# Exchanging the filler work of two stages, with fewer and larger transposing loads, in a fused forward and backward kernel

## The chip, the cores and the metric

The kernel runs on one core of a Trainium2 chip. The metric is the device time of one execution in microseconds (us). SBUF is the memory on the core, PSUM the small one, in banks, in which the matmuls leave their sums. The granted clock is the share of full speed at which PE was let run, as the profile records it. Engines are named as the profile names them: PE (matmul; PEld is its weight load), DVE (VectorE), ACT (ScalarE), POOL (GpSimd) and SP (SyncE, which issues most DMAs here; "SPq" is its queue). A program on one core has no die to compare, so a run of several rounds is called fast when it lies within 1.5% of the fastest of its kernel.

## The reference

The reference is the forward pass and all gradients of `x + A(LN(x)) + B(LN(x))` for S = 2048 rows, D = 512 columns, F = 1376 hidden columns, in bf16:

```python
def _A_ref(q, k, v, shift_k, ssm_k, ssm_D):
    k_shift = ...                       # causal 4-tap convolution of k with shift_k
    kv = k_shift * v
    y = irfft(rfft(kv padded to 4096) * rfft(ssm_k padded to 4096))[:2048] + kv * ssm_D
    return q * y
def _B_ref(x, w_gate, w_up, w_down):
    return ((x @ w_gate) * (x @ w_up)) @ w_down
xn = layernorm(x)
out = x + _A_ref(xn, ...) + _B_ref(xn, ...)   # and jax.vjp for all nine inputs
```

Ten outputs: out_0 the result; out_1, out_2, out_3 the gradients of x, k, v (2048 x 512); out_4 of shift_k (512 x 4); out_5 of ssm_k (512 x 2048); out_6 of ssm_D (512 numbers); out_7, out_8, out_9 of the three MLP weights.

## The kernel before

The long convolution is done as matmuls with generated sine tables. The program has four parts, and two of them are *paired*: the instruction streams of two independent jobs are woven together, so that PE always has matmuls of one job while the other waits for ACT or DVE.

1. MLP forward (`pg`, `pd`) over 8 chunks of 256 rows, with the first transform step (`pa`) between. It leaves three hidden tensors of every chunk in DRAM (`HDD`) and the transformed rows in DRAM (`AX`).
2. The **spectral step** (`pX`, pointwise products on DVE, `pC`), which reads `AX` and writes `CX`, paired with the **MLP backward matmuls** (`po`, `px`, 528 matmuls of 512 columns), which reread `HDD` chunk by chunk and leave their results in SBUF.
3. The **output stage** (`py`, `p5`, `psD` and most of the elementwise work), which reads `CX`, paired with the **weight gradients** (`pw`, 560 matmuls), which need the hidden tensors with rows and columns exchanged: 9 groups, each of 8 transposing loads.
4. The end of the output stage.

```python
def nat_load(n):                                  # transposing loads of group n
    t, g = glist[n]; fb0, nf = GRP[g]             # GRP = [(0, 4), (4, 4), (8, 3)] blocks of 128
    dst = f["nat"][n % 2]
    for ch in range(NCH):                         # 8 loads of 192 to 256 KB
        ldT(out=dst[:, ch, 0:nf, :]..., in_=HDD[ch, :, t, fb0:fb0 + nf, :]...)
...
st(HDD[ch], hd[ch % 2][:])                        # part 1: one store of a chunk, 16.9 KB per partition
...
while not SG.done:                                # part 2: spectral step + MLP backward
    SG(1)
    Y(5)
Y(1000)
f_alloc(); c_load(0)
nat_load(0)
while not (WG.done and CG.done):                  # part 3: weight gradients + output stage
    WG(12)
    CG(1)
```

At the end of the output stage, two outputs are stored element by element, and the sums for out_2 use one buffer:

```python
def dk_pair(r0):                                  # 4 products, 3 sums, one store of 256 KB
    dks = f["dks"]; acc = f["dk"]; ...
    st(o2[:, r0:r0 + 2, :], acc[:])
...
st(out_5.rearrange("(q p) s -> p q s", p=128), o5[:])
st(out_6.rearrange("(q p) -> p q", p=128), dD)            # 512 pieces of 2 bytes
st(out_4.rearrange("(q p) j -> p q j", p=128), ds4)       # 512 pieces of 8 bytes
```

## Time and profile before

| | kernel before |
|---|---|
| median at first (4 runs) | 617.23 us (613.73 to 619.96) |
| profiled span | 618.2 us |
| PE busy, DVE busy, ACT busy | 498.6, 357.1, 325.0 us |
| DMA | 146.85 MB, mean 238 GB/s |

The page of the kernel before has a row for each engine in which a digit is the busy share of one fortieth of the span, in tenths, and below them the granted PE clock and the DMA engines in the same form:

```profile
PE 498.6 (81%) x3040; PEld 258.0 (42%) x3084; DVE 357.1 (58%) x706; ACT 325.0 (53%) x403; POOL 7.7 (1%) x20
...
PE   0399999999998999999999989379699887795300
...
PEclk9999999999999999999999999879799989897655
DMA  8967867976956849756748997838999999987710
```

PE is full, or nearly, from the third slice to the twenty-fifth, then has holes, and the clock falls with them. The windows view gives busy time by stretch. Columns: window, its length, busy us (and instructions) of PE, PEld, DVE, ACT, POOL, then the granted clock, the mean busy share of the 16 DMA engines, and GB/s. A share above 1 comes from packet records that overlap, and is read as full. The four rows are part 1, part 2, part 3 until PE's last main work, and the end. They are cut by eye: the last matmuls of part 2 run to 362 us, and the last of the output stage, which wait for DVE, to 586:

```profile
core 0: us, PE busy (x) PEld busy (x) DVE busy (x) ACT busy (x) POOL busy (x), PEclk, DMA share, GB/s
0.00:184.50 184.50, 153.40 (x1340) 127.34 (x1358) 142.12 (x298) 130.12 (x199) 6.75 (x19) 1.00 0.79 270
184.50:356.00 171.50, 166.98 (x864) 53.94 (x879) 89.38 (x161) 111.84 (x126) 0.00 (x0) 1.00 0.73 248
356.00:577.00 221.00, 173.90 (x827) 75.92 (x837) 104.09 (x207) 79.39 (x75) 0.95 (x1) 0.90 0.91 231
577.00:618.20 41.20, 4.31 (x12) 0.76 (x11) 21.56 (x42) 3.63 (x4) 0.00 (x0) 0.50 0.23 84
```

Part 2 is bound by PE with DMA at 0.73. In part 3 PE idles 47 of 221 us, the clock is 0.90, and DMA is at 0.91 while it moves *fewer* bytes per second than in part 1. In the last 41 us there is hardly a matmul. The waits view (engine, line and tile, what it waited for; us in total, times, longest) names what PE waited for in part 3, and the timeline of the SP queue (start, us, line, what) shows why: eight transposing loads stand in front of the loads of the output stage.

```profile
PE py L602 <- DMA big<-CX: 27.0, 7, 13.4
...
PE psD L648 <- DVE big L646: 14.9, 9, 4.3
...
PE pw L712 <- DMA big<-HDD: 5.1, 6, 1.6
```

```profile
507.42 11.21 SPq L685 DMA_TRANSPOSE big<-HDD  x8
518.68 0.57 SPq L635 DMA_DIRECT2D out_dram<-big  x1
519.35 0.38 SPq L653 DMA_DIRECT2D out_dram<-big  x1
519.78 1.29 SPq L567 DMA_DIRECT2D big<-CX  x2
```

### The profile page before, as it was taken

The page shows a single profiled execution, that of the slowest core. Times are in us where ns is not written, and L with a number is a line of the kernel's source. Part 1 is how long each engine was busy: PE and PEld are TensorE (multiplying, and loading weights), DVE is VectorE, ACT ScalarE, POOL GpSimd, SP SyncE. Part 2 cuts the span into 40 slices and gives each one's busy share as a digit, 9 for nine tenths or more (in the row PEclk, how much of TensorE's full clock was granted, in tenths as well). Part 3 has the DMA queues.
Part 4 walks back from the last instruction along what each step waited for, and adds up shares of the span by engine and source line. Part 5 has one row for each costly group of instructions (what it writes and reads, how often), then busy time and mean ns, then how long its engine had stood idle before and what let it go on. Part 6 is the DMA issues. An engine that isn't in the chain of part 4 may idle for free. (4 is left out here: it accounts for less than half of the span.)

```text
span 618.2 us, 8204 instructions
## 1 busy us (share of the span) xinstructions
PE 498.6 (81%) x3040; PEld 258.0 (42%) x3084; DVE 357.1 (58%) x706; ACT 325.0 (53%) x403; POOL 7.7 (1%) x20
## 2 busy tenths in 40 slices
PE   0399999999998999999999989379699887795300
PEld 0297778787783333333333334133234423342100
DVE  4477999877863746464646317034266471639970
ACT  2076888789974866666666515042235340515500
POOL 2000010000000000000000000000000000000000
PEclk9999999999999999999999999879799989897655
DMA  8967867976956849756748997838999999987710
GB/s 294 329 135 279 316 232 287 372 282 200 313 193 278 312 162 317 261 203 242 290 151 290 226 295 179 181 99 184 276 239 255 302 201 223 261 241 279 273 43 9
DMA packets 124007, 146.85 MB, mean 238 GB/s; under 512 B 90240, under 2 KB 96192, under 8 KB 122047
## 3 DMA queue, kind: packets, MB, share of 16 engines
q1 hardware_dynamic: 122764, 142.99, 75.8%
q10 hardware_dynamic: 1202, 3.34, 1.5%
q8 instruction: 24, 0.39, 0.3%
q14 instruction: 17, 0.13, 0.1%
HBM read 65.30 MB, written 59.28 MB: 202 GB/s over the span
## 5 line engine op out<-in xcount | busy, mean ns | idle before, releaser
L712 PE MATMUL pw<-big 128*128 128x512 bf16 (+1 forms) x384 | 88.2, 379 | 7.8 <-DMA big<-HDD 5.1
L352 PE MATMUL pg<-big 128*128 128x256 bf16 (+1 forms) x704 | 88.9, 273 | 0.5
L352 PEld LDWEIGHTS <-big 128*128 128x128 bf16 (+1 forms) x704 | 69.5, 100 | 13.2 <-issue 0.2
L449 PE MATMUL px<-big 128*128 128x512 bf16 (+1 forms) x172 | 65.4, 380 | 0.9 <-issue 0.8
L447 PE MATMUL px<-big 128*128 128x512 bf16 (+1 forms) x169 | 64.3, 381 | 0.5 <-issue 0.5
L484 DVE TENSOR_TENSOR big<-big 128x2048 bf16<-128x2048 bf16 x16 | 19.6, 1225 | 76.2 <-ACT big L477 76.2
L477 ACT CAST big<-pX 128x1024 bf16<-128x1024 f32 x48 | 48.4, 1013 | 26.2 <-PE pX L476 19.0
L615 DVE TENSOR_TENSOR big<-big 128x1024 bf16<-128x1024 bf16 x8 | 5.5, 693 | 97.4 <-ACT big L603 97.4
L353 ACT CAST big<-pg 128x512 bf16<-128x512 f32 (+1 forms) x88 | 52.0, 604 | 17.3 <-PE pg L352 16.2
L508 ACT CAST big<-pC 128x1024 bf16<-128x1024 f32 x48 | 48.6, 1012 | 23.3 <-PE pC L507 20.8
L712 PEld LDWEIGHTS <-big 128*128 128x128 bf16 x384 | 37.4, 101 | 54.8 <-issue 23.9
L400 ACT CAST big<-pa 128x1024 bf16<-128x1024 f32 x48 | 48.2, 1034 | 5.2 <-PE pa L399 2.2
L359 PE MATMUL pd<-big 128*128 128x256 bf16 (+1 forms) x352 | 47.2, 273 | 1.0 <-ACT big L353 0.7
L441 PE MATMUL po<-big 128*128 128x512 bf16 (+1 forms) x169 | 44.1, 381 | 0.8 <-issue 0.6
L603 ACT CAST big<-py 128x1024 bf16<-128x1024 f32 x16 | 15.5, 1015 | 54.2 <-PE py L602 54.1
L716 ACT CAST big<-pw 128x512 bf16<-128x512 f32 (+1 forms) x24 | 14.5, 620 | 55.4 <-PE pw L712 37.0
L699 PE MATMUL pw<-big 128*128 128x512 bf16 (+1 forms) x172 | 42.0, 394 | 0.5 <-issue 0.4
L602 PE MATMUL py<-big 128*128 128x512 bf16 x58 | 19.7, 450 | 27.6 <-DMA big<-CX 27.0
L611 ACT CAST big<-p 128x1024 bf16<-128x1024 f32 x8 | 36.8, 4595 | 2.9 <-PE p L609 2.9
L359 PEld LDWEIGHTS <-big 128*128 128x128 bf16 (+1 forms) x352 | 34.8, 100 | 7.9 <-issue 0.9
L364 DVE TENSOR_TENSOR big<-big 128x1024 bf16<-128x1024 bf16 (+1 forms) x48 | 30.7, 640 | 4.4 <-ACT big L361 4.3
L648 PE MATMUL psD<-big 128*32 128x512 bf16 x64 | 20.7, 439 | 14.9 <-DVE big L646 14.9
(116 smaller groups left out, 662.5 us busy)
## 6 DMA issues: line engine op xcount, KB each, us to landing
HDD<-big SPq DMA_DIRECT2D x8, 2112.0 KB, 9.1
big<-HDD SPq DMA_DIRECT2D x6, 2112.0 KB, 8.9
AX<-big SPq DMA_DIRECT2D x16, 768.0 KB, 4.2
big<-AX SPq DMA_DIRECT2D x16, 768.0 KB, 5.1
CX<-big SPq DMA_DIRECT2D x16, 768.0 KB, 4.8
big<-CX SPq DMA_DIRECT2D x16, 768.0 KB, 6.1
out_dram<-big SPq DMA_DIRECT2D x32, 256.0 KB, 2.8
big<-in_A_v_dram SPq DMA_DIRECT2D x16, 256.0 KB, 7.9
```

What stands on the lines that cost most here:

```text
L352: MM(pg[:fw, j, :], lhsT=W[:, c, fb * 128:fb * 128 + fw], rhs=T[:, 0, c, :], start=(c == 0), stop=(c == 3))
L353: ACOPY(g[:fw, 0:2, i, :], pg[:fw])
L359: MM(pd[:fw, i, :], lhsT=WdT[:, c, fb * 128:fb * 128 + fw], rhs=T[:, 1, c, :], start=(c == 0), stop=(c == 3))
L400: ACOPY(a[:, :, t, :], pa[:])
L441: MM(po[:], lhsT=h[:fw, 0, fb, ss], rhs=wy["d"][:fw, fb, :], start=(fb == 0), stop=(fb == NFB - 1))
L447: MM(px[:], lhsT=h[:fw, 1, fb, ss], rhs=wy["g"][:fw, fb, :], start=(fb == 0), stop=False)
L449: MM(px[:], lhsT=h[:fw, 2, fb, ss], rhs=wy["u"][:fw, fb, :], start=False, stop=(fb == NFB - 1))
L477: ACOPY(X[:, t, :, :], px[:])
L508: ACOPY(C[:, :, pr, :], pc[:])
L611: ACOPY(o5v[:, :, r0:r0 + 2, :], p5[:])
L699: MM(pw[:fw, :], lhsT=nat[:, r // 2, b, (r % 2) * 128:(r % 2) * 128 + fw], rhs=go[:, r, :], start=(r == 0), stop=(r == R - 1))
L712: MM(pw[:, 0:nf * 128].rearrange("p (b s) -> p b s", b=nf), lhsT=xn[:, r, rows(q)], rhs=nat[:, r // 2, 0:nf, (r % 2) * 128:(r % 2) * 128 + ...
```

## The change

Its intent: put the weight gradients, with their transposing loads, beside the spectral step, where DMA has room; put the MLP backward matmuls beside the output stage, and let DVE read their sums straight from PSUM; make the transposing loads fewer and larger.

The core of the diff (cuts marked by `...`; buffers placed by hand, PSUM split by hand in each part):

```diff
-    HDD = dram.tile([NCH, 128, 3, NFB, CH], BF, name="HDD")
+    HDD = [dram.tile([3, 128, NCH, nf * CH], BF, name=f"HDD{g}") for g, (_, nf) in enumerate(GRP)]
...
     def nat_load(n):
-        for ch in range(NCH):
-            ldT(out=dst[:, ch, 0:nf, :]..., in_=HDD[ch, :, t, fb0:fb0 + nf, :]...)
+        for h in range(2):                      # 2 loads of 0.75 to 1 MB
+            w = 4 * nf * CH
+            dst = nat[:, h * w:h * w + w].rearrange("p (b q) -> p b q", q=128)
+            ldT(out=dst, in_=HDD[g][t, :, 4 * h:4 * h + 4, :].rearrange("p c s -> p (c s)"))
...
-                ACOPY(bdt["o"][:, r, :], po[:])            # part 2 of before: PSUM to SBUF
-                ACOPY(bdt["x"][:, r, :], px[:])
...
+        TT(m[:, rr, :], m[:, rr, :], po, op=ALU.add)       # DVE reads PSUM
+        STT(dxn[:, rr, :], e[:, rr, :], 1.0, px, op0=ALU.mult, op1=ALU.add, accum_out=s1[:, r:r + 1])
...
-                acc[0] += 0.68                             # pace of the pa work in part 1
+            global_acc[0] += 0.9 if ch >= 1 else 0
...
-    while not SG.done: SG(1); Y(5)
-    while not (WG.done and CG.done): WG(12); CG(1)
+    while not SG.done: SG(1); WG(16); ...                  # spectral step + weight gradients
+    ...
+    for n in range(NCH):                                   # output stage + MLP backward
+        y_o(n, 0); c_o5(n); y_x(n, 0); c_dsk(n); y_o(n, 1); ...; y_x(n, 1); ...
...
-            st(out_6.rearrange("(q p) -> p q", p=128), dD)
+            nc.scalar.dma_start(out_6.rearrange("(q p) -> p q", p=128), dD)
```

The spectral step also gets three input buffers in place of two and six `Y` buffers in place of four, `CX` loads go from three buffers to two, and out_4 goes to ACT's queue like out_6. `HDD` is now stored in three pieces per chunk. The order of the steps within the spectral step and within the output stage changes too, and the stores of out_6 and out_4 are now issued before the last stores of out_2, not after them.

## The prediction

> **What bounds the kernel now.** The windows view splits the 618 us span into four stages. (1) To 184 us: MLP forward and transforms, PE busy about 95% once started. (2) 184.5 to 356: the spectral step (pX, pC) with the MLP backward matmuls (po, px) as filler; PE is busy 167 of 171.5 us, granted clock 1.00, DMA 0.73: PE-bound. (3) 356 to 601.7: weight gradients (pw, fed by 72 transposing DMAs) mixed with the output stage (py, p, psD); PE is busy only 178 of 246 us at a mean clock of 0.86, while DMA is at 0.85 and near 1.0 between 450 and 550. The SP timeline shows each batch of eight transposes holding the queue 9 to 17 us, other loads behind; the waits view has PE py waiting 27 us for CX, and PE is idle from about 577 us. (4) 601.7 to 618: DVE finished; only o2 and the tiny element-wise stores land.
>
> **What the change does.** It swaps the fillers. Weight gradients (560 matmuls) fill the spectral stage; the backward matmuls (528) fill the output stage, whose DVE reads them from PSUM (32 PSUM-to-SBUF copies of 0.59 us leave ACT, their SBUF copies go). Transposes become 18 of 0.75 to 1 MB. PE does the same work; one more hd load (2.1 MB) appears, and HDD pieces shrink from 16.9 KB to 2 KB or 1.5 KB. Tables are built earlier and the tiny stores go to ACT's queue.
>
> **Cost.**
> Stage 1: unchanged, about 185 us, the A work only moves earlier.
> Stage 2: in the timeline back-to-back 512-column matmuls start 0.215 us apart (the Trainium skill, "TensorE: Matmul & The Clock Gate", section Back-to-back issue gap, has 518 cycles at 2.4 GHz; the trace agrees), so 560 cost about 117 us; the 96 pX/pC groups take 0.55 to 0.6 us each, about 56. PE-bound 173 us. DMA, from packet times in the trace: transposes 75 to 90 us (256-byte packets, median 18 ns, on 16 engines), AX and CX 67, the rest about 25: 165 to 185 us, so nearly co-limiting. A large weight transpose in stage 1 held SP 5.1 us and landed well later; short three-block groups may stall once or twice. I allow 187.
> Stage 3: PE 528 x 0.215 = 114, plus py, p and psD about 36: 150 us. DVE about 18 us per chunk, 147 in all; DMA 48 MB, about 147 us at the measured packet times. Three near-equal limits with cross-waits: about 21 us per chunk, 170 with the start.
> Tail after PE ends: 10 us of DVE, then stores, 16 in all.
> Sum: 185 + 187 + 170 + 16 = 558.
>
> **Predicted:** 558 us, 80% range 538 to 588. Faster by over 2%: 0.96; within 2%: 0.03; slower: 0.01.
>
> **What would confirm.** PE idle much lower from 185 us to the end; granted clock at 0.95 or more there; backward matmuls beside py and psD; 18 transposes; PE waits for CX under 10 us; no DVE-only stretch over 15 us; stage 2 at 175 to 200 us, stage 3 at 160 to 185.
>
> **What would break it.** Large transposes landing later than a group lasts (pw waiting for HDD in every group, stage 2 over 210 us); the CX loads, now without a spare buffer, arriving late because SP waits on DVE for stores (PE idle before py each chunk, clock falling); psD waiting for DVE at 3 us or more per chunk.

## The result and the profile after

The changed kernel takes 551.91 us (median of 11 runs, 549.03 to 553.66) beside 614.87 us for the kernel before (16 runs). The ratio is 0.8971, with a 95% interval of 0.8945 to 0.8996. Ratios here are the mean time of one kernel's fast runs over that of the other's of the same rounds, so they are not quite the ratio of the medians quoted.

The page of the changed kernel, in the same rows as before:

```profile
PE 478.4 (87%) x3050; PEld 264.2 (48%) x3084; DVE 362.7 (66%) x734; ACT 305.6 (56%) x371; POOL 7.6 (1%) x20
...
PE   0199999999999979999997899979999999999930
...
PEclk9999999999999989999999999999999999999975
DMA  8997678887675799999999999989888888889372
```

The windows view of the changed kernel; the rows are again parts 1, 2 and 3 (from the first `po`, 370 us) and the end:

```profile
0.00:187.00 187.00, 156.21 (x1333) 127.13 (x1346) 141.41 (x294) 129.93 (x198) 6.23 (x18) 1.00 0.79 267
187.00:370.00 183.00, 168.77 (x955) 71.12 (x961) 91.45 (x166) 109.89 (x133) 1.41 (x2) 0.99 1.07 287
370.00:529.00 159.00, 153.45 (x765) 65.93 (x779) 120.12 (x257) 64.99 (x41) 0.00 (x0) 0.99 0.83 288
529.00:549.80 20.80, 0.00 (x0) 0.00 (x0) 9.68 (x19) 0.81 (x1) 0.00 (x0) 0.54 0.32 38
```

The holes are gone. Parts 2 and 3 together take 342 us in place of 392.5, and the end 20.8 in place of 41.2; part 1 is 2.5 us longer. PE's busy time fell by 20 us though it runs the same matmuls: in the kernel before, part of it ran at the lower clock (e11 below, the old order with a clock of 0.98 in part 3, has 480.6 us). DMA work moved as intended: part 2 is now full (1.07), part 3 has room (0.83), and both move 287 to 288 GB/s. PE's waits for `CX` and `HDD`, from the waits view:

```profile
PE M L519 <- DMA big<-HDD: 3.3, 1, 3.3
...
PE M L532 <- DMA big<-HDD: 1.9, 2, 1.4
PE Q L616 <- DMA big<-CX: 1.6, 2, 1.1
```

(L519 and L532 are the weight gradients, L616 is `py`.) Of the 68.4 us that the profiled spans differ by, the old parts 2 and 3 gave 50.5 and the end 20.4; part 1 took 2.5 back. But the old end still holds matmuls of the output stage. Counted from the last matmul of any kind, the ends are 31.9 us (586.3 to 618.2) and 21.4 (528.5 to 549.8), so 57.8 us of the gain lie before that point and 10.6 after it.

### The profile page after: what moved, and what is told of

Same layout as the page of the kernel before. It is cut to its first block, busy times and chain, and to the rows that moved or that the text cites. A ratio compares the mean times of both kernels' runs of the same rounds, so it can differ in the third digit from the quotient of the medians.

```text
span 549.8 us, 8221 instructions
## 1 busy us (share of the span) xinstructions
PE 478.4 (87%) x3050; PEld 264.2 (48%) x3084; DVE 362.7 (66%) x734; ACT 305.6 (56%) x371; POOL 7.6 (1%) x20
## 4 chain that ended last, share of the span: by engine, by line
PE 51%; DMA 19%; DVE 13%; ACT 7%; SPq 6%; issue 4%; ACTq 0%; DVEq 0%
PE H L371 9%; PE K L689 8%; PE M L519 7%; PE M L532 6%; DMA out_dram<-big 6%; DMA big<-HDD 4%; PE H L378 4%; DMA CX<-big 3%; PE K L672 3%; SPq L202 3%; DMA big<-CX 3%; PE Q L445 2%; PE Q L418 2%; ACT big L419 2%; PE Q L471 2%
## 5 line engine op out<-in xcount | busy, mean ns | idle before, releaser
L371 PE MATMUL H<-big 128*128 128x256 bf16 (+1 forms) x704 | 91.0, 275 | 0.5 <-ACT big L380 0.2
L689 PE MATMUL K<-big 128*128 128x512 bf16 (+1 forms) x344 | 82.3, 379 | 0.3
L532 PE MATMUL M<-big 128*128 128x512 bf16 (+1 forms) x384 | 79.8, 362 | 1.9 <-DMA big<-HDD 1.9
L371 PEld LDWEIGHTS <-big 128*128 128x128 bf16 (+1 forms) x704 | 69.9, 101 | 14.7 <-issue 0.5
L372 ACT CAST big<-H 128x512 bf16<-128x512 f32 (+1 forms) x88 | 51.9, 606 | 19.2 <-PE H L371 17.5
L532 PEld LDWEIGHTS <-big 128*128 128x128 bf16 x384 | 36.0, 98 | 44.9 <-issue 10.7
L689 PEld LDWEIGHTS <-big 128*128 128x128 bf16 (+1 forms) x352 | 33.1, 98 | 42.6 <-issue 6.4
L697 ACT ACTIVATE big<-big 128x512 bf16<-128x512 f32 x16 | 13.0, 813 | 70.9 <-DVE big L696 70.9
L419 ACT CAST big<-Q 128x1024 bf16<-128x1024 f32 x48 | 47.9, 1036 | 6.2 <-PE Q L418 2.6
L378 PE MATMUL H<-big 128*128 128x256 bf16 (+1 forms) x352 | 48.2, 272 | 1.2 <-ACT big L372 1.0
L672 PE MATMUL K<-big 128*128 128x512 bf16 (+1 forms) x172 | 44.2, 390 | 3.2 <-ACT big L536 2.9
L519 PE MATMUL M<-big 128*128 128x512 bf16 (+1 forms) x170 | 40.9, 385 | 4.2 <-DMA big<-HDD 3.3
L378 PEld LDWEIGHTS <-big 128*128 128x128 bf16 (+1 forms) x352 | 34.6, 100 | 7.8 <-issue 1.6
L650 ACT CAST big<-Q 128x1024 bf16<-128x1024 f32 x8 | 36.8, 4596 | 2.2 <-PE Q L648 2.2
L446 ACT CAST big<-Q 128x1024 bf16<-128x1024 f32 x34 | 33.0, 1021 | 6.3 <-PE Q L445 6.0
L536 ACT CAST big<-M 128x512 bf16<-128x512 f32 (+1 forms) x24 | 13.0, 544 | 41.4 <-PE M L532 19.6
L472 ACT CAST big<-Q 128x1024 bf16<-128x1024 f32 x32 | 30.8, 1015 | 9.4 <-DMA CX<-big 8.5
L357 PE MATMUL Q<-big 128*128 128x128 bf16 x128 | 10.4, 242 | 26.0 <-DVE big L245 25.9
L380 ACT CAST big<-H 128x512 bf16<-128x512 f32 (+1 forms) x48 | 27.3, 570 | 5.8 <-PE H L378 5.7
L672 PEld LDWEIGHTS <-big 128*128 128x128 bf16 (+1 forms) x176 | 16.8, 99 | 28.0 <-issue 10.8
```

Source lines behind the costliest of these rows:

```text
L371: MM(pg[:fw, j, :], lhsT=W[:, c, fb * 128:fb * 128 + fw], rhs=T[:, 0, c, :], start=(c == 0), stop=(c == 3))
L372: ACOPY(g[:fw, 0:2, i, :], pg[:fw])
L378: MM(pd[:fw, i, :], lhsT=WdT[:, c, fb * 128:fb * 128 + fw], rhs=T[:, 1, c, :], start=(c == 0), stop=(c == 3))
L419: ACOPY(a[:, :, t, :], pa[:])
L446: ACOPY(X[:, t, :, :], px)
L472: ACOPY(C[:, :, pr, :], pc)
```

## The experiments

Two readings compete. **Theory A**: exchanging the fillers made the gain. **Rival B**: the fewer, larger transposes freed the SP queue and made it. A third, **rival C**, credits the PSUM reads that saved 32 copies on ACT. The prediction itself leaned on A.

### One part of the change at a time: e1, e2, e3

**e1_small_tr** is the changed kernel with the transposing loads made small again:

```diff
-        for h in range(2):
-            w = 4 * nf * CH
+        for h in range(NCH):
+            w = nf * CH
...
-            ldT(out=dst, in_=HDD[g][t, :, 4 * h:4 * h + 4, :].rearrange("p c s -> p (c s)"))
+            ldT(out=dst, in_=HDD[g][t, :, h, :])
```

> The new schedule with 72 transposing loads of 192 to 256 KB in place of 18 of 0.75 to 1 MB; all else as changed. Theory A (exchanging the two fillers made the gain): within 2% of the changed kernel, 545 to 563 us, stage 2 (weight gradients with the spectral step) 180 to 192 us, since 72 x 1.26 us of SP issue is about the 18 x 4.7 us of the large ones and the bytes are equal. Rival B (fewer, larger transposes freed the SP queue and made the gain): at least 585 us, with weight-gradient matmuls waiting for HDD in every group.

**e2_big_tr_old** is the kernel before with the change's `HDD` layout and its 18 large loads, all else old:

```diff
-    HDD = dram.tile([NCH, 128, 3, NFB, CH], BF, name="HDD")
+    HDD = [dram.tile([3, 128, NCH, nf * CH], BF, name=f"HDD{g}") for g, (_, nf) in enumerate(GRP)]
...                                            # stores and reloads of HDD in three pieces
-        for ch in range(NCH): ldT(...)         # 8 loads
+        for h in range(2): ldT(...)            # 2 loads, as in the change
```

> The kernel before with the HDD layout of the change and 18 large transposes; its schedule (backward matmuls with the spectral step, weight gradients with the output stage) is kept. Theory A: 598 to 618 us, a gain of at most 3%, the weight-gradient and output stage still DMA-bound with PE idle 50 us or more. Rival B: 585 us or less.

**e3_evict_y** is the changed kernel with the PSUM copies put back:

```diff
+        ACOPY(bo, po)
-        TT(m[:, rr, :], m[:, rr, :], po, op=ALU.add)
+        TT(m[:, rr, :], m[:, rr, :], bo, op=ALU.add)
...
+        ACOPY(bx, px)
-        STT(dxn[:, rr, :], e[:, rr, :], 1.0, px, ...)
+        STT(dxn[:, rr, :], e[:, rr, :], 1.0, bx, ...)
```

> The changed kernel with the 32 copies of po and px from PSUM to SBUF by ACT put back (0.59 us each, one buffer for each of the two), VectorE reading the copies. Theory A: reading PSUM directly is only a convenience, ACT is idle over half of that stage: 549 to 560 us. Rival C (the saved copies and the shorter hop made a good part of the gain): 565 us or more.

Measured (3 rounds, beside the kernel before on the same chip):

| run | us, median | ratio to before, 95% interval |
|---|---|---|
| e1: new pairing, small transposes | 572.1 | 0.9332 (0.9273 to 0.9390) |
| e2: old pairing, large transposes | 594.1 | 0.9697 (0.9634 to 0.9760) |
| e3: the change with the copies back | 552.83 | 0.9016 (0.8957 to 0.9074) |
| the change (its own rounds) | 551.91 | 0.8971 (0.8945 to 0.8996) |

Neither A nor B came out as written. The large transposes alone bring 3.0%, the rest of the change without them 6.7%, and together 10.3%: the two add up, and the larger part is the rest of the change. That rest is not the pairing alone: buffers, PSUM split, PSUM reads and the order of steps changed with it. e1 lost 20 us against the change, where theory A had allowed 11. The expectation compared the median issue times (72 x 1.26 and 18 x 4.7 us, 91 and 85 in all); summed over all loads, the `HDD` transposes hold the SP queue 128 us in e1 and 100 in the change. The windows view shows the loss in part 2 alone (first row; the second is part 3):

```profile
186.00:390.00 204.00, 177.09 (x952) 72.86 (x958) 91.08 (x166) 109.11 (x132) 1.41 (x2) 0.94 1.03 256
390.00:549.00 159.00, 154.30 (x765) 66.52 (x779) 119.78 (x256) 65.18 (x41) 0.00 (x0) 0.98 0.84 289
```

Part 2 takes 204 us in place of 183 and moves 256 GB/s in place of 287; part 3 is unchanged. ACT's copies of `pC` wait longer for `CX` stores to leave their buffers (waits view, e1 and then the change):

```profile
ACT big L472 <- DMA CX<-big: 27.5, 7, 7.5
...
ACT big L472 <- DMA CX<-big: 8.5, 2, 4.3
```

The stores stand behind transposes in the SP queue: from the end of the last copy to the issue of its store pass 5.2 us at the median in e1 and 2.4 in the change, while the stores land 5.6 and 6.2 us after issue. The Trainium skill, "DMA: Bandwidth & Descriptors", section Rules for kernel authors, asks for 1 MiB or more per DMA; the runs agree for transposing loads, by 3 to 4% of this kernel.

Rival C falls: putting the copies back costs nothing that these rounds resolve (the intervals overlap). DVE's add of a 128 x 512 tile (the `po` half) took 0.68 us from PSUM and 0.42 from SBUF, so there ACT was spared 0.59 us and DVE charged 0.26; the fused operation on `px` took 0.69 us either way. The skill ("VectorE: DVE Perf Modes", section The perf-mode tier table) has a tensor_tensor with a PSUM operand drop from 2x to 1x; the trace agrees in direction, with a ratio of 1.6.

### What the transposes cost in each place: e11, e6

Two kernels make only the first two of nine groups of transposing loads and keep everything else, so that out_7, out_8 and out_9 are wrong:

```diff
-            if n + 1 < len(glist):
-                nat_load(n + 1)
+            if n == 0:
+                nat_load(1)
```

**e11_old_nat_once** does it to the kernel before, **e6_nat_once** to the changed kernel.

> Wrong result on purpose (out_7, out_8, out_9). The kernel before, old schedule, but only the first two of nine groups of transposing loads are made; all matmuls, copies and stores stay. Theory A (the third stage, 356 us to PE's end at 577, is slowed by the transposes on the DMA engines and the SP queue): PE's end at 540 us or earlier. Rival F (the output stage's own ACT and VectorE chain, single buffers, sets its pace): PE's end at 560 us or later.

> Wrong result on purpose (out_7, out_8, out_9). The changed kernel with only the first two of nine groups of transposing loads. Its stage 2 lasts 183 us with PE busy 169 and the DMA share over 1. If DMA and the SP queue make the 10 to 14 us of PE idleness: stage 2 of 172 to 176 us. If PSUM buffers and the ACT copies do: 180 us or more.

Both were run once (566.05 and 538.41 us), so the profiled spans are compared. First e11, parts 2, 3 and the end, then e6, the same:

```profile
184.50:356.00 171.50, 166.56 (x861) 53.79 (x877) 90.00 (x163) 111.26 (x125) 0.00 (x0) 1.00 0.72 248
356.00:535.00 179.00, 160.59 (x845) 74.22 (x852) 116.03 (x229) 82.79 (x79) 0.95 (x1) 0.98 0.72 226
535.00:564.00 29.00, 0.00 (x0) 0.00 (x0) 11.43 (x21) 0.00 (x0) 0.00 (x0) 0.50 0.12 37
```

```profile
187.00:357.00 170.00, 165.53 (x941) 69.94 (x947) 90.81 (x164) 109.86 (x131) 1.41 (x2) 0.99 0.76 234
357.00:514.00 157.00, 152.91 (x771) 66.03 (x784) 120.08 (x257) 64.78 (x40) 0.00 (x0) 1.00 0.84 290
514.00:536.60 22.60, 0.00 (x0) 0.00 (x0) 9.85 (x19) 0.81 (x1) 0.00 (x0) 0.56 0.34 35
```

With six traces the cost of (seven of nine groups of) transposing loads can be set out by place and size, as profiled spans in us:

| | 72 small loads | 18 large loads | two groups only |
|---|---|---|---|
| old pairing (beside the output stage) | 618.2 | 591.5 | 564.3 |
| new pairing (beside the spectral step) | 571.7 | 549.8 | 536.6 |

(The two groups kept are 16 small loads in the old pairing and 4 large ones in the new, so the costs are approximate.) The same loads cost 54 us (small) or 27 (large) beside the output stage, and 35 or 13 beside the spectral step. So theory A's mechanism is shown: the transposes were most of what made PE wait in the old part 3, and beside the spectral step more of them is hidden. But it gives only 19 us (54 to 35) or 14 (27 to 13). The larger part of what the change gives at equal load size (46.5 or 41.7 us) is the 28 us by which the old pairing stays longer without most transposes. These traces say where the 28 lie, not which edit brought them: 14 are PE idleness in part 3 (18 us, here 4; in e11's waits view `psD` waits 10.0 us for DVE there and `py` 5.1 for `CX`), 8 the end after the last matmul (30.7 us, here 22.9), and 5.5 PE's busy time. Rival F, that the output stage's own chain sets the pace, is refuted as the main cause (PE's end came at 535 us, not at 560), but the waits for DVE belong to it. The new order of steps, the buffers and the earlier issue of the last stores were not tested one by one.

### What bounds part 3 now: e7, e8

**e7_half_px** drops 176 of the backward matmuls, **e8_no_hd** drops six of seven reloads of hidden chunks:

```diff
-        for t, w in ((1, "g"), (2, "u")):        # e7: only ((1, "g"),)
...
-            if n + 2 < NCH:                       # e8
-                hd_load(n + 2)
```

> Wrong result on purpose (out_1). The changed kernel without the w_up half of px: 176 matmuls of 0.215 us, 38 us of PE time, fewer in stage 3; all else stays. If PE alone bounds stage 3 (159 us, PE busy 153): stage 3 falls by 25 us or more, to the next limit. If VectorE and DMA were near-equal limits, as predicted (147 us each): it stays at 148 us or more.

> Wrong result on purpose (out_0, out_1). The changed kernel without the last six of its seven reloads of hidden chunks in stage 3: 12.7 MB, about 38 us of DMA engine time, fewer. If PE alone bounds stage 3: it stays within 3 us of 159. If DMA bounds it too: it falls by 6 us or more.

Each was run once: 547.04 and 546.85 us. (The outputs are wrong by construction, yet both were reported correct: out_0 and out_1 stayed within the tolerance, presumably because other terms dominate them.) In e7, from the first `py` to the last `psD`, part 3 runs from 362.5 to 518.0 us, 155.5 us; in the change from 364.5 to 525.2, 160.7. 38 us of PE time removed gave back 5. In e8 the last `px` comes 158 us after the first `py`, in the change 162: about 32 us of DMA engine time removed (a share of 0.64 of 156 us in place of 0.83 of 159) gave back 4 (3 by the windows view). The expectation had 3 at most for "PE alone" and 6 or more for "DMA too", so e8 decides nothing by itself. e7 does: PE alone doesn't bound part 3, though it is busy 153 of 159 us. From 369 to 519 us e7 has PE busy 123 of 150 us and DVE 117, and PE now waits for the DVE read of `po` to free its bank:

```profile
PE K L689 <- DVE big L674: 16.7, 6, 3.3
```

Part of what e7 didn't give back is the clock: it fell to 0.91 from 427 us on, and PE's busy time in the stretch fell by 27 us (152.9 to 126.2), not by 38. So a limit stands within a few us behind PE, as "three near-equal limits" has it, but the prediction's sums for DVE and DMA (147 us each) are not borne out: DVE was busy 120 us, and DMA's share makes 132. Which of DVE's chain, the CX loads and the SP queue comes next was not separated.

### The end and the start: e5b, e10, e12, e13, e14

The end of the changed kernel is 20.8 us and was predicted at 16. The timeline of its DVE and queues shows it stopped for 7.8 us by a store. (L719 stores out_4, L700 out_1, L608 the sums for out_2.)

```profile
525.22 0.41 ACTq L710 DMA_DIRECT2D out_dram<-big  x1
...
530.25 0.40 ACTq L719 DMA_DIRECT2D out_dram<-big  x1
...
532.61 0.33 SPq L700 DMA_DIRECT2D out_dram<-big  x1
...
533.93 13.18 SPq L608 DMA_DIRECT2D out_dram<-big  x2
...
542.43 0.69 DVE L605 TENSOR_TENSOR big<-big 128x1024 bf16<-128x1024 bf16 x1 [7.80 <-DMA out_dram<-big]
```

L710, the store of out_6, lands late itself. The list of DMA issues gives KB and the us from issue to landing of out_6 (1 KB) and out_4 (4 KB):

```profile
out_dram<-big ACTq DMA_DIRECT2D x1, 1.0 KB, 16.4
out_dram<-big ACTq DMA_DIRECT2D x1, 4.0 KB, 11.6
```

The kernel before has the same store of out_6 on SP's queue. It was issued at 601.9 us, when DVE was done, and landed at 617.1 of 618.2: in its last 16 us no engine works, and only these last stores are still to land.

```profile
out_dram<-big SPq DMA_DIRECT2D x1, 1.0 KB, 15.1
```

**Theory D**: these two, 512 pieces of 2 bytes and 512 of 8, hold up the writes behind them. **Rival E**: the stores wait behind the 2 MB of out_5, or the single buffer of the out_2 sums is the cost. Three edits of the changed kernel, each alone, then together:

```diff
# e10_elem
-            nc.scalar.dma_start(out_6.rearrange("(q p) -> p q", p=128), dD)          # at the end
+        if ch == 0:                                                                  # after its column is complete
+                nc.scalar.dma_start(out_6.rearrange("(q p) -> p q", p=128), f["o5"][:, :, 0])
-            nc.tensor.transpose(pt[:, q, :], dsb[:, rows(q)], ident[:])
+            nc.tensor.transpose(pt[:, q, :], dsb[:, q::4], ident[:])
-            nc.scalar.dma_start(out_4.rearrange("(q p) j -> p q j", p=128), ds4)     # 8-byte pieces
+            nc.scalar.dma_start(out_4.rearrange("(p q) j -> p q j", q=4), ds4)       # 32-byte pieces
# e5b_dk2
-        acc = f["dk"]
+        acc = f["dk2"][(r0 // 2) % 2]
# e12_start
-    ldT(out=WdT[:], in_=B_w_down)
     xload(1)
+    ldT(out=WdT[:], in_=B_w_down)
# e13_best: all three
```

> The changed kernel with the two element-wise stores mended: out_6 (512 pieces of 2 bytes) sent after the first finished chunk of column 0 in place of the end, out_4 in 128 pieces of 32 bytes in place of 512 of 8. In the changed kernel the last 21 us hold no matmul, and the 256 KB o2 store issued at 533.9 us right after these two lands only at 542.4, its 2 KB packets taking up to 5 us each in place of 0.09. Theory D (the tiny writes stall the writes behind them): the tail after the last matmul falls from 21 us to 13 or 14, total 541 to 545 us. Rival E (the stores wait behind the 2 MB out_5, or the single dk buffer alone costs it): 548 us or more.

> The changed kernel with a second buffer for the dk sums, so that the last dk_pair needn't wait for the store of the one before. Rival E (single dk buffer): tail falls to about 14 us, total 541 to 545 us. Theory D: VectorE ends 8 us earlier, but its last stores still queue behind the stalled ones, so the end moves by 0 to 5 us: 545 to 552 us.

> The changed kernel with the second x load issued before the 16.7 us transposing load of w_down on the SP queue. Both kernels start PE at 25.9 us because VectorE, in order, waits at 12 to 23.8 us for that second x load before it may finish the first layernorm. If that is right, PE starts 6 to 11 us earlier and the total falls to 540 to 546 us; if the weights or w_down's transpose were the real limit of the start, the total stays at 549 us or more.

> All three together: element-wise stores mended, two dk buffers, second x load first. If the three are independent: 530 to 539 us.

Measured (5 rounds):

| run | us, median | ratio to before, 95% interval |
|---|---|---|
| e10_elem | 558.17 | 0.9022 (0.8984 to 0.9059) |
| e5b_dk2 | 549.45 | 0.8900 (0.8872 to 0.8928) |
| e12_start | 548.88 | 0.8891 (0.8855 to 0.8927) |
| e13_best | 551.11 | 0.8902 (0.8856 to 0.8948) |

e10 missed: it became no faster. Its end did shrink (last matmul issued at 539.1 us of 555.6, a tail of 16.5 us where the change has 23.0), out_4 landed in 1.4 us, and the out_2 store that had taken 8 us landed in 2. But 12 us were lost in mid-stage (first `py` to last `px`: 173.9 us, in the change 162.3), just after out_6 was now sent. The timeline of e10 (PE, and the ACT queue's store of out_6), and the windows view around it:

```profile
400.44 0.41 ACTq L653 DMA_DIRECT2D out_dram<-big  x1
...
404.73 4.70 PE L692 MATMUL K<-big 128*128 128x512 bf16 x21
...
416.41 1.03 PE L616 MATMUL Q<-big 128*128 128x512 bf16 x2 [6.98 <-DMA big<-CX]
```

```profile
380.00:400.00 20.00, 19.12 (x99) 8.28 (x100) 12.82 (x30) 8.44 (x6) 0.00 (x0) 1.00 0.90 278
...
406.00:412.00 6.00, 3.43 (x16) 1.37 (x14) 1.84 (x4) 0.00 (x0) 0.00 (x0) 0.96 0.23 13
412.00:418.00 6.00, 1.59 (x4) 0.58 (x5) 0.10 (x1) 0.00 (x0) 0.00 (x0) 0.50 0.37 19
418.00:424.00 6.00, 4.38 (x14) 1.67 (x14) 2.24 (x7) 0.70 (x1) 0.00 (x0) 0.69 0.31 73
...
424.00:444.00 20.00, 19.12 (x99) 8.31 (x100) 14.13 (x31) 8.39 (x7) 0.00 (x0) 1.00 0.96 339
```

From 406 to 418 us the core's DMA engines move 13 to 19 GB/s, where they move 278 before and 339 after. The `CX` loads that hang there come from another queue (SP) than the 1 KB store (ACT), and are reads of DRAM, not writes. The packet records show more: the 512 packets of 2 bytes are all recorded between 404.2 and 405.6 us, 9 ns each, but the 6 KB packets of the `CX` loads just behind them, 0.23 us at the median otherwise, take up to 15.4 us, and the traffic recovers when out_6 lands, at 421.6. So the miss shows theory D more plainly than a hit would have: from the last two-byte packet to the landing of out_6 pass 13 us in the change, 14 in the kernel before and 16 in e10, and in the change and e10 the DMA that is pending behind it hangs until then; at the end of the kernel that is only less harmful. The Trainium skill, "DMA: Bandwidth & Descriptors", section Issuing engines are not separate DMA queues, says that all queues share the same 16 engines, and the trace agrees. Section Specifications says that below 512 bytes the engine does a read-modify-write. No run here shows that this is the cause: pieces of 32 bytes (out_4 in e10, landed in 1.4 us) are below 512 bytes too and held up nothing. Whether the size of the pieces or their number is what counts was not separated.

e5b brought a small gain (0.7 to 0.8% in the ratio, other rounds than the change's): as theory D had it, DVE ends earlier and its stores still queue. e12 fell short of its expectation: its first MLP matmul comes at 23.8 us in place of 29.8, so the load order was the limit of the start, but of these 6 us 5.6 are left at the end of part 1 and 2.6 at the last matmul; part 2, whose DMA share is 1.07 in e12 too, takes about half of it back. e13 held e10's stall as well, and so gained nothing over e12.

The last run, **e14_best**, keeps the second buffer, the load order and the 32-byte pieces, and turns out_6 on PE:

```diff
-            nc.scalar.dma_start(out_6.rearrange("(q p) -> p q", p=128), dD)
+        nc.tensor.transpose(p6, dD, ident[:])          # [128, 4] to [4, 128]
+        VCOPY(d6, p6)
+        nc.scalar.dma_start(out_6.rearrange("(q p) -> q p", p=128), d6)   # 4 rows of 256 bytes
```

> The changed kernel with out_6 turned by one small PE transpose and stored as 4 rows of 256 bytes at the end, out_4 in 32-byte pieces, two dk buffers, and the second x load issued first. Theory D (512 writes of 2 bytes hold up every DMA behind them for 10 to 17 us, at the end in the changed kernel, in the middle of stage 3 in the run that sent out_6 early): no stall in either place, tail after the last matmul 12 to 14 us in place of 21, total 533 to 543 us. Rival (out_4's pieces or the last plain stores stall by themselves, or the start's gain is lost again in the DMA-bound stage 2): 546 us or more.

Measured: 537.48 us, ratio 0.8744 (0.8713 to 0.8776), correct, against 0.8971 for the change: 2.5% less. The end in its windows view:

```profile
523.00:537.50 14.50, 2.02 (x12) 0.90 (x10) 9.91 (x22) 1.40 (x2) 0.00 (x0) 0.69 0.32 119
```

From the last `px` matmul's start to the end are 13.4 us (524.1 to 537.5) where the change has 23.0 (526.8 to 549.8). e13 differs from e14 in out_6 alone, so the two (of other rounds) give its price: 0.8902 against 0.8744, 1.8%. Rival E's part of it is small: out_5 still goes out as one 2 MB store in front, and the second buffer alone brought less than 1%.

## Why the prediction was right or wrong

- **Time.** 558 us was predicted (538 to 588); measured 551.91. The direction and size were right, with some luck: by the parts below, the errors are +2, -4, -11 and +5 us and partly cancel.
- **Mechanism.** "It swaps the fillers", with part 2 before PE-bound and DMA at 0.73, part 3 before held by the transposes in the SP queue: shown by e11 (part 3 without most transposes has 18 us of PE idleness in place of 47) and by the table of spans. The prediction treated the larger transposes as a detail; e1 shows that they make 22 us (571.7 to 549.8) of the 68.4 us that the profiled span shrank by, about a third, and e2 27 (618.2 to 591.5) in the old pairing. Nor does it name the 28 us that the new schedule gains without most transposes; their cause stays open.
- **Part 1**: 185 us predicted, 187 measured. **Part 2**: 187 predicted, 183 measured; that DMA would be co-limiting is shown by its share of 1.07 and by e6, where it falls to 170 us without most transposes (e6 doesn't separate the DMA engines from the SP queue). "PE-bound 173" was right in itself: PE was busy 169.
- **Part 3**: 170 predicted, 159 measured. PE's sum was right (150 predicted, 153 busy). The term that was mis-sized is DVE, "about 18 us per chunk, 147 in all": it was busy 120 us. The durations of the single instructions add up to 137 us, more than the busy time because they overlap: one of 128 x 1024 takes 0.69 us, but in an unbroken run the next starts 0.60 us after it starts, in the kernel before too. If the estimate added up durations, which it doesn't say, that is 17 of the 27 us; the other 10 stay open. DMA's term, 147, was 132. A limit close behind PE still held, by e7, with less cross-waiting: about 20 us per chunk in place of 21.
- **The end**: 16 us predicted, 20.8 measured. The term "then stores" was mis-sized: it did not see that the element-wise stores hold up the 256 KB stores behind them, and so DVE for 7.8 us. The kernel before had the hint: its out_6 store, too, landed 15.1 us after its issue. The prediction lists the move to ACT's queue without a cost; from there the store landed no sooner (16.4 us).
- **Confirmations named.** Clock of at least 0.95 after 185 us: 0.99 in parts 2 and 3. 18 transposes: yes. PE waits for `CX` under 10 us: 1.6. Part 2 in 175 to 200 us: yes. Part 3 in 160 to 185: 159 from the first `po`, just outside, or 164 from the first `py` (364.5 us) to the last matmul, inside. "No DVE-only stretch over 15 us": wrong, 20.8 us without a matmul remain, by the stall just told.
- **Named risks.** None of the three occurred: `pw` waited 5 us for `HDD` in all, `py` 1.6 for `CX`, and `psD` 1.6 for DVE (14.9 before).

## What to carry to other kernels

When two jobs are paired to fill each other's gaps, pair by the scarcest shared resource: here both pairings keep PE fed by count of matmuls, but only one keeps the DMA-heavy job away from the other DMA-heavy job, which hid 14 to 19 us more of the transposes. In a DMA-full stage the size of each transposing load matters as well as the bytes, since plain loads and stores stand behind them in the issuing queue. Look for stores in pieces of a few bytes before anything else at a kernel's end, and turn them on PE into rows; sending them earlier or from another queue moves the stall, and can make it dearer.

## What the Trainium skill lacked or had wrong

- "DMA: Bandwidth & Descriptors", sections Specifications and Rules for kernel authors: the read-modify-write below 512 bytes is named, its effect on other traffic of the same core is not. 1 KB in 512 pieces of 2 bytes landed 13.5 to 21.2 us after issue, and in e10 held the DMA of the core, reads too, to 13 to 19 GB/s for about 12 us and to 73 in the next 6. Pieces of 32 bytes (4 KB in all) landed in 1.4 us in place of 11.6 for 8-byte pieces sent behind the 2-byte ones, and caused no stall that the trace shows.
- The same page, section Latency and other measured facts, has 261 GB/s for transposing loads of one kind and 350 to 400 for contiguous ones; no run here isolates that rate. The page gives no figure for the cost of their issue: here a load of 192 to 256 KB held the SP queue 1.26 to 1.33 us at the median and one of 0.75 to 1 MB 4.7, and the large ones saved 3 to 4% of the whole kernel with the same bytes.
- "TensorE: Matmul & The Clock Gate", section Back-to-back issue gap: its formula for a matmul of 512 columns (518 cycles) agrees with the 0.215 us spacing seen here; the lower "sustained" figure of 131 ns for pairs of weight load and matmul, which the same section gives, was not reached in the runs of matmuls of 512 columns here.
- Nothing else in the runs spoke against these pages.
